# One pair's transposes moved from TensorE to DMA, and one sum of values moved to GpSimd, in a routed attention with a gated feed-forward

## The chip, the core and the metric

The kernel runs on one core of a Trainium2 chip. The metric is the device time of one execution in microseconds (us); a time is the median of several runs. The core has five instruction queues: PE (TensorE, matrix products), DVE (VectorE), ACT (ScalarE), POOL (GpSimd) and SP (SyncE, which here only issues DMAs). Each queue runs its own instructions strictly in the order in which they were built; queues wait for each other by semaphores.

## The reference

Four batches of eight heads, 768 positions, head size 64, sixteen centroids. Each query and key is assigned to its nearest centroid, and a query sees only keys of its own cluster. The result goes through a gated feed-forward.

```python
q_assign = argmax(einsum('bhsd,hcd->bhsc', q_n, c_n))      # k_assign in the same way
mask = q_assign[:, :, :, None] == k_assign[:, :, None, :]
scores = where(mask, scale * q @ k.T, -1e9)
attn_out = softmax(scores) @ v                             # (4, 8, 768, 64)
x = attn_out.transpose(0, 2, 1, 3).reshape(3072, 512)
out = (sigmoid(x @ w_gate) * (x @ w_val)) @ w_out          # (3072, 512) f32
```

## The kernel before

**Heads and tiles.** Heads are handled in pairs, four to a batch. For each head there is a tile `T` of 128 rows by 12 blocks of 128 columns: six blocks of keys, six of queries, each transposed. A number is stored as two f16 halves: `hi`, a cast, and `lo`, the f32 value minus `hi`; rows 0 to 63 of T hold hi and 64 to 127 lo. They stand in a tile `hl` first, not transposed. Once the cluster logits (`lg`, a product of T with the centroids `cm`) are taken, sixteen of the lo rows (64 to 79) are overwritten with the one-hot rows of the cluster (`oh`: for keys 1 at the cluster, for queries -1920 at every other one), so that one product of keys and queries gives a score with its mask already in it.

**Steps.** The attention runs in steps. One step is one score product `sc` (L1066, 128x384) on PE, one exponential `es` on ACT (L1071) and, two or three steps later, three products `av` (L1089) with the values `va`. After the last step of a pair DVE adds the sum of values `sv` and takes a reciprocal `rec` (L384, L389), POOL multiplies (`xp`, L390), and `xp` is turned to `xTb`, by PE (`x_ps`, L1117, copied by DVE at L1118) or by a DMA on SP (L1120). `sv` is 1e-30 times the column sum of the values, so that a query whose cluster holds no key gets their mean; the sum is made by a product with ones: either six products over `va` (`v_sum_pe`, L356) or three adds on f32 values and then one product (`v_sum`, adds L332, L338 and L339, product L343).

**The first batch** takes its queries in two halves of three blocks: the four pairs with the first half are steps 0 to 47, the same pairs with the second half are steps 48 to 95. Its preparation is done on PE (`first`, and `rest` for the second half of the queries: `hl2`, L1411 and L1415). From the second batch on, step 96 onwards, a pair takes 24 steps.

**Two ways to prepare a later pair.** `pieces` (L1159 to L1267) is the way on PE: the casts at L1171, the subtractions at L1178, twelve transposes a head by PE into `t_ps` (L1198), copied into T by DVE (L1211) or ACT (L1209), logits (L436), one-hots (L1226, L1229), six transposes a head for the one-hots into `oh_ps` (L1250), copied into T by DVE (L1261) and ACT (L1263). `pair_prep` is the way by DMA:

```python
DVE.tensor_copy(hl[:, :, 0:64], r)                                          # L1631
POOL.tensor_tensor(hl[:, :, 64:128], r, hl[:, :, 0:64], ALU.subtract)       # L1632
SP.dma_start_transpose(out=T[key], in_=hl.rearrange("p c x -> p (c x)"))    # L412
# logits L436, then on DVE: L451 (sum of two halves), L462 (max), L464 twice (one-hots), L471 (scale)
SP.dma_start_transpose(out=st["ot"], in_=st["oh"].rearrange("p c x -> p (c x)"))   # L1649
SP.dma_start(out=t[64:80, c0 : c0 + n, :], in_=src[32 * slot : 32 * slot + 16, 0:n, :])  # L492, four times
```

The number `npe` of the table `SCHED` says for how many pairs of the second batch the first way is taken: one, its first pair. All other pairs of the second to the fourth batch go by DMA.

**The feed-forward** of a block of 384 tokens is cut into groups of four products: `g` (L532, then a tanh `th` on ACT) and `v` (L548, then `hT` on DVE, L553), and after these the output products `o` (L865, L994). They are filled in between the steps by a credit in ns for each step (`ns..` in the table). The weights come by DMAs that POOL issues (L252, and L259 for `wo`).

**What sets the order.** Everything is written out by hand: `SCHED` holds, for each named piece of work, the step behind which it is built into the queues (for later batches as an offset from the first step of the pair, which is step 96 for the first pair of the second batch). PSUM has a ring of four banks that `sc`, `g`, `v`, `lg` and `x_ps` share: a product waits until the reader of the bank that it gets is done. `hl` has four buffers, T eight, the one-hot tile `oh` three.

Of the kernel before, what the change touches and what calls it, by code (L numbers as in the profile page):

```python
# [19 lines left out]
]  # L20
SCHED = {
# [74 lines left out]
    "fwv": [354, 356, 357, 359, 364, 366, 370, 371], "b3p2pk1": -28.5, "END": 0,  # L96
}


# [1671 lines left out]
```

## Time and profile before

| | |
|---|---|
| median of 3 runs | 319.33 us (319.31 to 320.36) |
| profiled execution | 319.12 us, of which the span from first to last instruction is 317.3 us |
| PE busy | 310.0 us (98%) |
| ACT, DVE, POOL busy | 244.9, 238.6, 120.9 us |
| step 48 / step 96 begin (sc) | 35.86 us / 73.36 us |
| granted TensorE clock | 1.00 |

The span's times count from its first instruction. A row of the timeline has start, duration, engine, line, operation, what is written from what, shapes, and how many follow each other; in brackets is how long the engine idled before and what ended it. Matmuls overlap in the pipeline, so a row's duration is longer than the time until the next one starts.

### The profile page before, as it was taken

What the parts mean: (1) busy time and instruction counts of PE and PEld (TensorE: products, weight loads), DVE (VectorE), ACT (ScalarE), POOL (GpSimd) and SP (SyncE); (2) the same over time, 40 slices, a digit from 0 to 9 for tenths busy, and PEclk for the clock granted to TensorE, in tenths of its full rate; (3) what the DMA queues carried; (4) which work ended last, traced back from release to release, by engine and by line L of the source; (5) the groups of instructions that cost most, each with busy time, mean ns of one, the idle gap of its engine ahead of it and who ended that gap; (6) DMA issues with size and microseconds to landing.
All of it is one profiled execution on the core that took longest, in us unless ns stands there. A gap on an engine that the chain in (4) does not pass through costs nothing.

```text
span 317.3 us, 9228 instructions
## 1 busy us (share of the span) xinstructions
PE 310.0 (98%) x3492; PEld 218.8 (69%) x3492; DVE 238.6 (75%) x623; ACT 244.9 (77%) x555; POOL 120.9 (38%) x157
## 2 busy tenths in 40 slices
PE   7899999999999999999999999999999999999995
PEld 4688766766666666666777678766677678656685
DVE  5899756778688777686788688776888776678983
ACT  6688998797899887877776876777877887588621
POOL 5888454244434275423234333424212111026600
PEclk9999999999999999999999999999999999999999
DMA  7999998639848988976676455882506130300014
GB/s 196 379 259 169 271 164 143 176 83 264 242 100 163 204 221 136 199 217 161 106 193 153 151 118 134 248 153 53 112 2 76 55 27 14 145 1 3 0 35 165
DMA packets 77996, 45.16 MB, mean 142 GB/s; under 512 B 56896, under 2 KB 75520, under 8 KB 77952
## 3 DMA queue, kind: packets, MB, share of 16 engines
q1 hardware_dynamic: 73840, 39.66, 51.3%
q0 software_dynamic: 3680, 4.72, 9.1%
q8 instruction: 27, 0.44, 0.6%
q10 hardware_dynamic: 432, 0.20, 0.2%
q14 instruction: 17, 0.14, 0.1%
HBM read 28.34 MB, written 6.29 MB: 109 GB/s over the span
## 4 chain that ended last, share of the span: by engine, by line
PE 93%; DMA 2%; DVE 1%; POOL 1%; SPq 1%; issue 0%; ACT 0%; DVEq 0%
PE sc L1066 19%; PE g L532 15%; PE v L548 15%; PE av L1089 11%; PE o L994 9%; PE o L865 5%; PE lg L436 2%; PE o L699 2%; PE o_end L802 2%; PE av L699 2%; DMA kraw<-in_k_dram 2%; PE v L628 2%; PE y L699 2%; PE o L802 1%; PE av L802 1%; PE z L699 1%
## 5 line engine op out<-in xcount | busy, mean ns | idle before, releaser
L1071 ACT ACTIVATE es<-sc 128x384 f16<-128x384 f32 x384 | 174.1, 492 | 38.5 <-PE sc L1066 29.8
L1066 PE MATMUL sc<-T 128*128 128x384 f16 x384 | 117.3, 325 | 0.7 <-DVE T L1396 0.4
L1089 PEld LDWEIGHTS <-es 128*128 128x128 f16 x1152 | 81.3, 98 | 35.1 <-ACT es L1071 0.2
L1089 PE MATMUL av<-va,es 128*128 128x65 f16 x1152 | 97.6, 194 | 0.0
L553 DVE SCALAR_TENSOR_TENSOR hT<-th,v 128x384 f16<-128x384 f32 x72 | 39.8, 553 | 33.8 <-PE av L1089 29.6
L377 POOL TENSOR_TENSOR xp<-t,rec 128x384 f16<-128x384 f32 (+1 forms) x30 | 21.8, 726 | 97.3 <-DVE rec L374 49.2
L548 PE MATMUL v<-xTb,wv 128*128 128x384 f16 x288 | 58.5, 326 | 0.1
L532 PE MATMUL g<-xTb,wg 128*128 128x384 f16 x288 | 58.5, 326 | 0.0
L538 ACT ACTIVATE th<-g 128x384 f32<-128x384 f32 x72 | 35.4, 492 | 8.3 <-PE g L532 6.3
L1066 PEld LDWEIGHTS <-T 128*128 128x128 f16 x384 | 37.0, 96 | 1.2 <-DVE T L1396 0.7
L548 PEld LDWEIGHTS <-wv 128*128 128x128 f16 x288 | 28.0, 97 | 13.9 <-issue 0.3
L532 PEld LDWEIGHTS <-wg 128*128 128x128 f16 x288 | 27.9, 97 | 13.9
L1632 POOL TENSOR_TENSOR hl<-kraw,hl 128x384 f16<-128x384 f32 x22 | 20.2, 920 | 40.6 <-DVE hl L1631 25.9
L1632 POOL TENSOR_TENSOR hl<-qraw,hl 128x384 f16<-128x384 f32 x22 | 21.1, 961 | 11.1 <-DVE hl L1631 11.1
L865 PE MATMUL o<-wo,hT 128*128 128x512 f16 x72 | 19.9, 379 | 0.0
L372 DVE TENSOR_TENSOR t<-av,sv 128x390 f32<-128x390 f32 (+1 forms) x30 | 14.4, 480 | 7.1 <-PE av L1089 5.3
L941 DVE TENSOR_TENSOR ob<-o,ob 128x256 f32<-128x256 f32 (+1 forms) x28 | 15.0, 549 | 4.7 <-PE o L994 3.2
L708 POOL TENSOR_TENSOR hT<-T 128x384 f16<-128x384 f32 x12 | 11.8, 1001 | 16.2 <-DVE T L657 15.6
L994 PE MATMUL o<-wo,hT 128*128 128x256 f16 x108 | 16.8, 272 | 0.0
L994 PEld LDWEIGHTS <-sum 128*128 128x128 f16 x144 | 14.0, 97 | 3.3
L451 DVE TENSOR_REDUCE lgs<-lg 128x192 f32<-128x384 f32 x23 | 12.7, 551 | 3.0 <-PE lg L436 2.9
L324 POOL CAST va<-vraw 128x768 f16<-128x768 f32 x15 | 13.1, 873 | 2.4 <-DMA vraw<-in_v_dram 2.4
(225 smaller groups left out, 470.2 us busy)
## 6 DMA issues: line engine op xcount, KB each, us to landing
vraw<-in_v_dram SPq DMA_DIRECT2D x15, 384.0 KB, 4.9
kraw<-in_k_dram SPq DMA_DIRECT2D x14, 384.0 KB, 4.2
qraw<-in_q_dram SPq DMA_DIRECT2D x12, 384.0 KB, 4.1
out_dram<-ob SPq DMA_DIRECT2D x17, 256.0 KB, 2.2
wg<-in_moe_w_gate_dram POOLq DMA_DIRECT2D x2, 768.0 KB, 9.2
wv<-in_moe_w_val_dram POOLq DMA_DIRECT2D x2, 768.0 KB, 10.4
wo<-in_moe_w_out_dram POOLq DMA_DIRECT2D x2, 768.0 KB, 9.3
T<-ohT SPq DMA_DIRECT2D x44, 24.0 KB, 1.9
```

Source lines behind the costliest of these rows:

```text
L377: (eng or POOL).tensor_tensor(x, t[:, 0:nq, 0:64], bcast(rec[:, 0:nq], 64), ALU.mult)
L532: PE.matmul(out=g[:, 0:n], lhsT=wg[fc // WQ][:, dc, fc % WQ, :], rhs=xT[:, dc, t0 : t0 + n], start=(dc == 0), stop=(dc == NDC - 1),)
L538: ACT.activation(th[:, 0:n], g[:, 0:n], AF.Tanh)
L548: PE.matmul(out=w[:, 0:n], lhsT=wv[fc // WQ][:, dc, fc % WQ, :], rhs=xT[:, dc, t0 : t0 + n], start=(dc == 0), stop=(dc == NDC - 1),)
L553: DVE.scalar_tensor_tensor(HB[b, blk][:, fc, 0:n], st[0][:, 0:n], 1.0, w[:, 0:n], ALU.add, ALU.mult)
L699: PE.matmul(out=o, lhsT=l, rhs=r, start=start and d == 0, stop=stop and d == 1, skip_group_check=True,)
L865: PE.matmul(out=o, lhsT=HB[b, blk][:, fc, bass.ts(t, 128)], rhs=wo[fc // WON][:, fc % WON, :], start=(fc == 0), stop=(fc == NFC - 1),)
L994: PE.matmul(out=st[z][:, e], lhsT=a[:, c, :], rhs=rhs[:, c, :], start=start and c + e == 0, stop=c == HF - 1, skip_group_check=True,)
L1066: PE.matmul(out=sc.rearrange("p (c t) -> p c t", t=128), lhsT=s["k"], rhs=s["q"], start=True, stop=True,)
L1071: ACT.activation(es, sc, AF.Exp, scale=SCALE)
L1089: PE.matmul(out=av[:, a0 + s["c0"] + i, :], lhsT=s["es"][:, bass.ts(i, 128)], rhs=VA[b, p][:, e, s["j"], :], start=(first and i == 0 and a ...
L1632: POOL.tensor_tensor(hl[:, :, 64:128], r, hl[:, :, 0:64], ALU.subtract)
```

## The change

Only the table `SCHED` changes.

```diff
-    "halved1": 1, "halved0": 4, "npe": 1, "npe0": 4, "vs00": 4.5, "gb": 0, "rb": 0, "h1hi0":
+    "halved1": 1, "halved0": 4, "npe": 0, "npe0": 4, "vs00": 4.5, "gb": 0, "rb": 0, "h1hi0":
...
-    75.5, "r3ot": 78.0, "r3pl0": 81.5, "r3pl1": 82.5, "ql3": -1, "vc03": 30.0, "vs03": 31.5,
+    75.5, "r3ot": 78.0, "r3pl0": 81.5, "r3pl1": 82.5, "ql3": -1, "vc03": 30.0, "vs03": 37,
...
-    "fwv": [354, 356, 357, 359, 364, 366, 370, 371], "b3p2pk1": -28.5, "END": 0,
+    "fwv": [354, 356, 357, 359, 364, 366, 370, 371], "b3p2pk1": -28.5, "b1p0sp00": -38, "b1p0sp01": -37, "b1p0sp10": -36, "b1p0sp11": -35, "b1p0tn0": -33.5, "b1p0tn1": -31, "b1p0lg0": -26, "b1p0pk0": -25, "b1p0lg1": -22, "b1p0pk1": -21, "b1p0ot": -19.5, "b1p0hp0": -13, "b1p0hp1": -12, "vd3": 1, "vq3": 1, "vt03": 6, "END": 0,
```

With `npe` at 0 the first pair of the second batch goes by DMA as well: 24 transposes of `hl` and 12 of `oh` leave PE, two T transposes, a one-hot transpose and four row copies are added to SP's queue. Its splits stand at steps 58 to 61 (before, 68 to 85), its transposes at 62.5 and 65, its logits at 70 and 74. `vd3`, `vq3` and `vt03` make the sum of values of the first batch's last pair by three adds on POOL and one product at step 43, where six products on PE stood at step 31.5.

The first place is POOL's queue around the xp of the first pair's second half (the first L390 after the `wo` DMAs in each piece; it is the one that x_ps of step 66 reads). Before:

```order
L259 DMA wo_120<-in_moe_w_out_dram 128x6x512
L1411 COPY hl_1280<-qheld 128x6x64
L259 DMA wo_121<-in_moe_w_out_dram 128x6x512
L1632 TENSOR_TENSOR hl<-kraw,hl 128x6x64
L390 TENSOR_TENSOR xp<-t,rec 128x2x3x64
L1415 TENSOR_TENSOR hl_1280<-qheld,hl_1280 128x6x64
L1632 TENSOR_TENSOR hl<-qraw,hl 128x6x64
```

And in the change:

```order
L259 DMA wo_120<-in_moe_w_out_dram 128x6x512
L1632 TENSOR_TENSOR hl<-kraw,hl 128x6x64
L1411 COPY hl_1283<-qheld 128x6x64
L1632 TENSOR_TENSOR hl<-qraw,hl 128x6x64
L1632 TENSOR_TENSOR hl<-kraw,hl 128x6x64
L259 DMA wo_121<-in_moe_w_out_dram 128x6x512
L1632 TENSOR_TENSOR hl<-kraw,hl 128x6x64
L1632 TENSOR_TENSOR hl<-qraw,hl 128x6x64
L390 TENSOR_TENSOR xp<-t,rec 128x2x3x64
L1415 TENSOR_TENSOR hl_1283<-qheld,hl_1283 128x6x64
```

Four more subtractions stand ahead of xp, and the second `wo` DMA stands behind three of them. PE's queue has x_ps at the same place in both, right behind the score product of step 66.

The second place is DVE's queue at the same steps; the difference:

```order
-L553 TENSOR_SCALAR hT<-th,v 128x384 x2
-L1631 COPY hl<-kraw 128x6x64
+L553 TENSOR_SCALAR hT<-th,v 128x384
+L1631 COPY hl<-kraw 128x6x64
+L1631 COPY hl<-qraw 128x6x64
+L553 TENSOR_SCALAR hT<-th,v 128x384
+L1631 COPY hl<-kraw 128x6x64 x2
+L1631 COPY hl<-qraw 128x6x64
```

The casts that POOL's subtractions wait for stand behind the first and the second hT.

The third place is DVE's queue at steps 71 to 76, in the change, from an hT over the two one-hot chains of the turned pair (L451 to L471, into `oh_136`) to the next two hT's; the chain at L1451 and L1452 is that of the last pair's second half, and PE turns its result `oh_134`:

```order
L553 TENSOR_SCALAR hT<-th,v 128x384
L384 TENSOR_TENSOR t<-av,sv 128x390
L389 RECIPROCAL rec<-t 128x6
L453 TENSOR_TENSOR lgs<-lg,lglo 128x96
L451 TENSOR_REDUCE lgs<-lg 128x192
L462 TENSOR_REDUCE mx<-lgs 128x12
L464 TENSOR_TENSOR oh_136<-lgs,mx 128x6x16 x2
L471 TENSOR_SCALAR oh_136<-oh_136 128x6x16
L1451 TENSOR_REDUCE mx<-lgs 128x6
L1452 TENSOR_TENSOR oh_134<-lgs,mx 128x2x3x16
L553 TENSOR_SCALAR hT<-th,v 128x384 x3
```

Before, the same piece has no L451 to L471 between L453 and L1451:

```order
L553 TENSOR_SCALAR hT<-th,v 128x384
L384 TENSOR_TENSOR t<-av,sv 128x390
L389 RECIPROCAL rec<-t 128x6
L453 TENSOR_TENSOR lgs<-lg,lglo 128x96
L1451 TENSOR_REDUCE mx<-lgs 128x6
L1452 TENSOR_TENSOR oh_136<-lgs,mx 128x2x3x16
L553 TENSOR_SCALAR hT<-th,v 128x384
```

The other one-hot chain of the turned pair, with two casts of the next pair behind it, stands just ahead of this piece in the change, also between two hT's.

## The prediction

> **What bounds the kernel now.** I read the page first, its totals and its chain that ended last:
>
> ```profile
> PE 310.0 (98%) x3492; PEld 218.8 (69%) x3492; DVE 238.6 (75%) x623; ACT 244.9 (77%) x555; POOL 120.9 (38%) x157
> ...
> PE 93%; DMA 2%; DVE 1%; POOL 1%; SPq 1%; issue 0%; ACT 0%; DVEq 0%
> ```
>
> TensorE is busy 98% of the span and is 93% of the chain. Then I read the two stretches that the change touches, in the table by windows:
>
> ```profile
> 30.00:40.00 10.00, 9.51 (x165) 7.21 (x163) 7.13 (x22) 9.56 (x25) 4.63 (x7) 1.00 1.07 253
> ...
> 60.00:70.00 10.00, 10.00 (x121) 6.73 (x120) 8.15 (x24) 9.02 (x20) 3.55 (x4) 1.00 0.59 143
> ```
>
> Columns: length, then busy us of PE, PEld, DVE, ACT and POOL, then clock and DMA. From 40 us on TensorE never pauses, so every matmul removed there is time won, and every wait put on TensorE is time lost. At 30 to 40 us ScalarE (9.56) binds as much as TensorE (9.51). The order of each engine is fixed at build, so a wait cannot be stepped around.
>
> **What goes.** The grouped rows and the timeline of PE:
>
> ```profile
> L1198 PE MATMUL t_ps<-identh,hl 128*128 128x128 f16 x24 | 2.0, 219 | 0.0
> ...
> L1250 PE MATMUL oh_ps<-identh,oh 128*128 128x128 f16 x12 | 1.0, 219 | 0.0
> ```
> ```profile
> 28.27 0.51 PE L356 MATMUL vs_ps<-va,ones 128*128 128x130 f16 x6
> 28.62 0.33 PE L1117 MATMUL x_ps<-identh,xp 128*128 128x128 f16 x3
> ...
> 34.12 0.32 PE L1066 MATMUL sc<-T 128*128 128x384 f16 x1
> ...
> 55.19 0.50 PE L1198 MATMUL t_ps<-identh,hl 128*128 128x128 f16 x6
> 55.52 0.81 PE L548 MATMUL v<-xTb,wv 128*128 128x384 f16 x4
> ```
>
> Durations overlap in the pipeline, so the cost is from start to start: six transposes hold TensorE 55.52 - 55.19 = 0.33 to 0.34 us. The 24 + 12 = 36 removed cost 6 x 0.335 = **-2.01 us**, all in stretches where TensorE binds. [...] The rows say 0.056 us apiece at granted clock 1.00, and they decide. The logits matmuls (L436) stay, 24 of them; they only move.
>
> **The sum of values.** Six matmuls go, one comes: 0.35 - 0.06 = 0.29 us of TensorE at 28.3 us. In its place GpSimd does three adds, which no row shows on GpSimd; the nearest are its 128x384 subtract (0.91) and the same adds on VectorE (0.55 for the first). The first add fits into the 1.46 us that GpSimd idles before 32.66 (row below). The other two follow that xp, which ends at 33.48; at 0.3 to 0.45 apiece they end at 34.1 to 34.4. The single ones-matmul stands right before the score matmul of 34.12, so after a gain of 0.29 TensorE waits there 0.2 to 0.5, and ScalarE, back to back then, hides part of it. Bounds -0.3 to +0.3; I take **0**, as gain and wait are the same size.
>
> **The wait that comes: GpSimd.** What precedes the attention output xp of the first pair's second half on GpSimd:
>
> ```profile
> 32.66 0.82 POOL L390 TENSOR_TENSOR xp<-t,rec 128x384 f16<-128x384 f32 x1 [1.46 <-DVE rec L389]
> ...
> 37.76 0.82 POOL L390 TENSOR_TENSOR xp<-t,rec 128x384 f16<-128x384 f32 x1 [3.83 <-DVE rec L389]
> 38.54 0.91 POOL L1415 TENSOR_TENSOR hl<-qraw,hl 128x384 f16<-128x384 f32 x1
> 39.40 0.89 POOL L259 DMA_DIRECT2D wo<-in_moe_w_out_dram  x1
> 40.28 0.52 POOL L1411 CAST hl<-qheld 128x384 f16<-128x384 f32 x1
> 40.73 0.82 POOL L259 DMA_DIRECT2D wo<-in_moe_w_out_dram  x1
> 44.46 0.91 POOL L1632 TENSOR_TENSOR hl<-kraw,hl 128x384 f16<-128x384 f32 x1 [2.91 <-DVE hl L1631]
> 45.67 0.82 POOL L390 TENSOR_TENSOR xp<-t,rec 128x384 f16<-128x384 f32 x1 [0.30 <-DVE rec L389]
> 46.45 1.03 POOL L1415 TENSOR_TENSOR hl<-qheld,hl 128x384 f16<-128x384 f32 x1
> ```
>
> Start to start a subtract takes 0.86, a wo load 0.88, the cast 0.45. In the changed order the xp now at 45.67 stands behind five subtracts, the cast and the second wo load. All of them follow the first of the new VectorE casts, which stands behind the first hT:
>
> ```profile
> 41.41 0.56 DVE L553 SCALAR_TENSOR_TENSOR hT<-th,v 128x384 f16<-128x384 f32 x1 [2.03 <-PE av L1089]
> 43.55 0.55 DVE L553 SCALAR_TENSOR_TENSOR hT<-th,v 128x384 f16<-128x384 f32 x1 [1.58 <-PE av L1089]
> 44.02 0.35 DVE L1631 CAST hl<-kraw 128x384 f16<-128x384 f32 x1
> ...
> 52.56 0.35 DVE L1171 CAST hl<-qraw 128x384 f16<-128x384 f32 x1
> 52.83 0.35 DVE L1631 CAST hl<-kraw 128x384 f16<-128x384 f32 x1
> ```
>
> A cast starts 0.47 after an hT (43.55 to 44.02) and GpSimd 0.44 after the cast's start (44.02 to 44.46): 41.41 + 0.47 + 0.44 = 42.32. Then 5 x 0.87 + 0.45 + 0.85 = 5.65: xp starts at 47.97 and ends at 48.79. TensorE needs it for x_ps:
>
> ```profile
> 38.64 0.34 PE L1117 MATMUL x_ps<-identh,xp 128*128 128x128 f16 x3
> ...
> 46.90 0.33 PE L1117 MATMUL x_ps<-identh,xp 128*128 128x128 f16 x3
> ```
>
> The earlier pair shows the coupling: xp 37.76 + 0.82 = 38.58, x_ps at 38.64, 0.06 later. Here x_ps can start at 48.85 instead of 46.90: **+1.95 us**. Bounds: 1.7 (each link a little shorter) to 2.6 (each subtract 1.03, as the one at 46.45). Queued behind x_ps is all of TensorE.
>
> **The second wait: VectorE.** The two logits blocks of the turned pair come at steps 70 and 74 instead of 79 and 92, so both one-hot chains and two casts fall between two hT. Rows for the pieces:
>
> ```profile
> 54.15 0.55 DVE L553 SCALAR_TENSOR_TENSOR hT<-th,v 128x384 f16<-128x384 f32 x1 [0.70 <-PE av L1089]
> 54.62 0.56 DVE L384 TENSOR_TENSOR t<-av,sv 128x390 f32<-128x390 f32 x1
> ...
> 56.44 0.55 DVE L553 SCALAR_TENSOR_TENSOR hT<-th,v 128x384 f16<-128x384 f32 x1
> ...
> 62.77 0.56 DVE L451 TENSOR_REDUCE lgs<-lg 128x192 f32<-128x384 f32 x1
> ...
> 64.31 0.55 DVE L553 SCALAR_TENSOR_TENSOR hT<-th,v 128x384 f16<-128x384 f32 x1
> ```
> ```profile
> 51.17 0.81 PE L548 MATMUL v<-xTb,wv 128*128 128x384 f16 x4
> ...
> 53.23 0.81 PE L548 MATMUL v<-xTb,wv 128*128 128x384 f16 x4
> ...
> 67.44 0.45 PE L436 MATMUL lg<-cm,T 128*128 128x32 f16 x12
> 67.74 0.32 PE L1066 MATMUL sc<-T 128*128 128x384 f16 x1
> ```
>
> One chain (reduce, max, two one-hots, scale) takes 64.31 - 62.77 = 1.54; the chain t, reciprocal, sum, max, one-hot 56.44 - 54.62 = 1.82; casts 0.27 apart (52.56 to 52.83); an hT 0.47. An hT follows its v by 0.92 (53.23 to 54.15). Count from the v that stands at 53.23. The hT before it began 2.06 earlier, so this one begins at -2.06 + 0.92 + 0.47 + 1.54 + 0.54 = 1.41 instead of 0.92, and ends at 1.96. After it come 0.47 + 1.82 + 1.54, so the rest rows' one-hots (oh) end at 5.24. TensorE gets to its transpose of them (oh_ps) at 4.17: it adds g and v (0.65 each), sc 0.165, av 0.09, and the block of 12 logits 0.30. With 0.06 for the semaphore it waits 5.30 - 4.17 = **+1.13**, part of it already at the g that needs the late hT's bank. Bounds 0.6 (VectorE 10% quicker) to 1.6 (10% slower).
>
> **The queue of SyncE.** The turned tiles themselves are in time: issued near 44.6 and 48.0, landing 3.8 us later, used near 52.9 and 56.3. Later the next pair's second tile is late: its transpose follows an xT transpose, three loads and now the one-hot transpose too.
>
> ```profile
> 59.33 2.42 SPq L412 DMA_TRANSPOSE T<-hl  x1
> ```
> ```profile
> T<-hl SPq DMA_TRANSPOSE x4, 3.8
> ```
> ```profile
> T<-hl SPq DMA_TRANSPOSE x1, 6.2
> ```
>
> (The 3.8 is the median of 20 to 60 us, the 6.2 the one behind three loads.) Its xp moves by about 3.0 us with VectorE, the added transpose is about 1.2: issue at 63.5, landing at 69.7. The logits that read it (67.44) move by 1.95 + 1.13 + 0.30 for a logits block that comes forward, less 4 x 0.335 removed by then, to 69.5. **+0.2**, bounds 0 and 0.9.
>
> **Sum.** -2.01 + 0 + 1.95 + 1.13 + 0.2 = +1.3. The profiled execution took 319.12 (span 317.3 and 1.8 around it), 0.2 below the median of 319.33; added to the median: **320.6**. Four evictions leave ScalarE and four VectorE; TensorE waits for none of them now, so that is worth nothing. All low bounds at once give 319.3 and all high ones 322.7; as they hardly fall together, the forecast's own range is 319.6 to 321.7.
>
> **Rivals.** *The waits stay hidden*: only the 2.0 are left, 317.3. For it: GpSimd idles 2.91 before 44.46 and the four added subtracts cost 3.5, which nearly fits. Against: the casts stand behind hT, so 0.9 of that idle time cannot be used, and the slack between xp and x_ps is only 46.90 - 46.49 = 0.4. Chance 0.13.
>
> *The late tile decides, slower*: the place is the block of logits at 67.44, which reads the next pair's second tile. SyncE issues the transpose of that tile behind the xT transpose, three loads and the added one-hot transpose. The price is 1 us for each us that it lands after 69.5, so it decides once the transpose is issued after about 63.3 (69.5 - 6.2). With 1.0 to 1.8 for loads that now share the transfer engines with one transpose more: 321.6 to 322.4. Against: only 0.2 is worked out above. Chance 0.17.
>
> *GpSimd is blocked by VectorE*: the subtract at 46.45 took 1.03 beside a busy VectorE against 0.91 elsewhere. If each of the five loses a whole hT or cast (0.35 to 0.55), the chain grows by 1.7 to 2.7: 322.3 to 323.3. Against: no row has more than 0.25 of it. Chance 0.08. [...]
>
> That the change does not do what it says is excluded by the built order.
>
> **How the numbers follow.** Forecast 0.62, hidden 0.13, late tile 0.17, blocked 0.08. A measurement of this kernel can tell 0.5%, 1.6 us, from no change: 317.7 to 320.9. A third of the forecast's band lies above 320.9. Faster 0.13; slower 0.17 + 0.08 + 0.21 = 0.46; the same 0.41. The range leaves out the hidden case and the far end of the others: 318.8 to 322.4.
>
> **What would show it.** TensorE's waits should have a new row of about 2 us at x_ps, L1117, for xp, L390, near 47 us, and 1 us of waits for VectorE at g and oh_ps near 57 to 61 us; busy PE falls by about 2. If x_ps starts within 0.5 us of its old place after sc, the GpSimd step is wrong; if the VectorE chain ends before oh_ps is reached, that step is. [...]

## The result and the profile after

The changed kernel takes **323.87 us** (median of 6 executions, 321.77 to 325.40) against 319.32 (318.80 to 320.36): a ratio of 1.0137, 95% interval 1.0090 to 1.0184. It is slower, above the range of 318.8 to 322.4. The profiled execution took 322.40, its span is 320.6 (before: 319.12 and 317.3).

The six executions fall in two groups by mean granted clock. Two ran at 1.000 (322.40 and 321.77, mean 322.1), four at 0.994 to 0.995 (323.06 to 325.40, mean 324.6). The profile below is one of the first group: the second has a cost of its own, which experiments 2, 8 and 11 show.

The page of the profile after, its totals and its chain:

```profile
PE 308.8 (96%) x3451; PEld 216.5 (68%) x3451; DVE 238.4 (74%) x621; ACT 241.8 (75%) x550; POOL 124.2 (39%) x161
...
PE 84%; DMA 5%; POOL 4%; issue 2%; DVE 2%; ACT 1%; SPq 1%; DVEq 0%; POOLq 0%
```

TensorE has 41 matmuls fewer, but the part of the chain on it fell from 93% to 84%: DMA, GpSimd and VectorE now end waits. What TensorE waits for (total, times, longest):

```profile
PE lg L436 <- DMA T<-hl: 1.7, 2, 1.4
PE x_ps L1117 <- POOL xp L390: 1.6, 1, 1.6
...
PE sc L1066 <- DVE hT L553: 0.6, 1, 0.6
...
PE vs_ps L343 <- ACT es L1071: 0.2, 1, 0.2
PE g L532 <- ACT th L538: 0.2, 1, 0.2
```

None of these five rows exists before. The three long ones in TensorE's timeline:

```profile
47.15 0.32 PE L1066 MATMUL sc<-T 128*128 128x384 f16 x1 [0.62 <-DVE hT L553]
...
47.40 0.33 PE L1066 MATMUL sc<-T 128*128 128x384 f16 x1
49.33 0.34 PE L1117 MATMUL x_ps<-identh,xp 128*128 128x128 f16 x3 [1.60 <-POOL xp L390]
...
56.78 0.23 PE L436 MATMUL lg<-cm,T 128*128 128x32 f16 x3
58.43 0.54 PE L436 MATMUL lg<-cm,T 128*128 128x32 f16 x15 [1.42 <-DMA T<-hl]
```

The start of the same score product, after minus before, is a running account of what the change has cost (us):

| step | 32 | 44 | 65 | 67 | 72 | 75 | 84 | 100 | 188 | end |
|---|---|---|---|---|---|---|---|---|---|---|
| shift | -0.29 | -0.11 | 0.67 | 2.38 | 2.81 | 4.70 | 3.52 | 2.64 | 3.04 | 3.3 |

The -0.29 stands from step 20 on, ahead of everything that the change moves, so up to step 44 the sum of values costs 0.18. Each later jump is one wait and a little more: 0.78 for the wait of 0.62, 1.71 for the one of 1.60. Of the 0.43 between 67 and 72, 0.30 is the first block of logits that comes forward. Of the 1.89 between 72 and 75, 1.42 is the wait and 0.30 the second block. Behind step 75 the 36 transposes that are gone (2.0) and the two blocks of logits that already ran (0.6) give back 2.06, 0.55 less than they should: 0.35 of that is lost at the g behind step 85 (67.67), which waits 0.18 for ScalarE's `th`, and 0.12 at the logits at 71.04, whose tile lands at 70.99.

**GpSimd's chain** ahead of xp, its queue in order of time:

```profile
42.21 0.95 POOL L1632 TENSOR_TENSOR hl<-kraw,hl 128x384 f16<-128x384 f32 x1 [2.04 <-DVE hl L1631]
43.11 0.50 POOL L1411 CAST hl<-qheld 128x384 f16<-128x384 f32 x1
43.57 0.91 POOL L1632 TENSOR_TENSOR hl<-qraw,hl 128x384 f16<-128x384 f32 x1
44.77 0.96 POOL L1632 TENSOR_TENSOR hl<-kraw,hl 128x384 f16<-128x384 f32 x1 [0.29 <-DVE hl L1631]
45.68 0.86 POOL L259 DMA_DIRECT2D wo<-in_moe_w_out_dram  x1
46.56 0.92 POOL L1632 TENSOR_TENSOR hl<-kraw,hl 128x384 f16<-128x384 f32 x1
47.44 0.91 POOL L1632 TENSOR_TENSOR hl<-qraw,hl 128x384 f16<-128x384 f32 x1
48.30 0.97 POOL L390 TENSOR_TENSOR xp<-t,rec 128x384 f16<-128x384 f32 x1
```

It begins at 42.21 (forecast 42.32) and reaches xp at 48.30 (forecast 47.97).

**VectorE beside it**, in the same microseconds and once later:

```profile
44.88 1.07 DVE L1631 CAST hl<-qraw 128x384 f16<-128x384 f32 x1
...
46.57 0.53 DVE L553 SCALAR_TENSOR_TENSOR hT<-th,v 128x384 f16<-128x384 f32 x1
...
47.18 1.42 DVE L1631 CAST hl<-qraw 128x384 f16<-128x384 f32 x1
...
56.91 0.35 DVE L1631 CAST hl<-kraw 128x384 f16<-128x384 f32 x1
```

A cast of 0.35 (56.91, GpSimd idle) takes 1.07 and 1.42 here. Each ends 0.2 to 0.25 after a GpSimd operation ends (45.73, 48.35). The hT behind the first of them is late, and sc at 47.15 waits for it: a wait that was not in the prediction.

**SyncE's queue**: the turned pair's second transpose (L412) and the first transpose of the last pair's second half (L1422), after; then L1422 before:

```profile
48.37 3.37 SPq L412 DMA_TRANSPOSE T<-hl  x1
...
51.84 1.21 SPq L1422 DMA_TRANSPOSE T<-hl  x1
```

```profile
47.51 1.28 SPq L1422 DMA_TRANSPOSE T<-hl  x1
```

The issue of a transpose holds SyncE for 3.37 us where the others from 44 to 56 us hold it 1.2 to 1.7, and L1422 stands behind it: issued 4.3 us later than before. The logits of the last pair's second half (3 + 3 matmuls, the x3 at 56.78 and the first three of the x15) are what waits 1.42: the second L1422, issued at 53.09, lands at 58.38, where before it landed at 52.25.

### The profile page after: what moved, and what is told of

It reads as the page before. It is cut to its first block, busy times and chain, and to the rows that moved or that the text cites. A ratio compares the mean times of both kernels' runs of the same rounds, so it can differ in the third digit from the quotient of the medians.

```text
span 320.6 us, 9159 instructions
## 1 busy us (share of the span) xinstructions
PE 308.8 (96%) x3451; PEld 216.5 (68%) x3451; DVE 238.4 (74%) x621; ACT 241.8 (75%) x550; POOL 124.2 (39%) x161
## 4 chain that ended last, share of the span: by engine, by line
PE 84%; DMA 5%; POOL 4%; issue 2%; DVE 2%; ACT 1%; SPq 1%; DVEq 0%; POOLq 0%
PE sc L1066 17%; PE g L532 13%; PE v L548 13%; PE av L1089 9%; PE o L994 9%; PE o L865 4%; DMA T<-hl 4%; PE o L699 2%; PE lg L436 2%; PE o_end L802 2%; PE av L699 2%; DMA kraw<-in_k_dram 2%; PE v L628 2%; PE y L699 2%; PE o L802 1%
## 5 line engine op out<-in xcount | busy, mean ns | idle before, releaser
L1632 POOL TENSOR_TENSOR hl<-kraw,hl 128x384 f16<-128x384 f32 x24 | 22.2, 926 | 40.5 <-DVE hl L1631 25.3
L1632 POOL TENSOR_TENSOR hl<-qraw,hl 128x384 f16<-128x384 f32 x24 | 22.9, 955 | 11.4 <-DVE hl L1631 11.4
L451 DVE TENSOR_REDUCE lgs<-lg 128x192 f32<-128x384 f32 x23 | 12.7, 552 | 1.9 <-PE lg L436 1.8
```

## The experiments

Three theories were to be told apart for the waits. **Queues**: each wait comes from one named queue position. **Full engines**: VectorE, SyncE and GpSimd have no room here, and a wait that is removed only moves. And for the clock: **a pause of TensorE of about 2 us makes the granted clock fall**, or chance does. Each run's own kernel before, on the same chip, had a median between 318.8 and 319.4.

### 1. The sum of values alone, in the kernel before

```diff
-    "vs03": 31.5,
+    "vs03": 37, "vd3": 1, "vq3": 1, "vt03": 6,
```

> Only the sum of values on GpSimd, the pair as before. My account (the loss comes from the pair's splits ahead of xp on GpSimd): TensorE gains 0.3 us at the place of the six matmuls and gives it back where it waits for the adds or ScalarE, so within 0.5 us of the kernel before, x_ps of step 66 within 0.3 us behind xp, granted clock 1.00 in all runs. Rival (the adds on GpSimd delay what follows them): 1 us or more slower, with a wait before the first hT.

319.28 us (10 executions), ratio 1.0009 (0.9997 to 1.0021). The product waits 0.2 for ScalarE. The gain of 0.25 at step 33 is gone at step 44, where the kernel is 0.17 later than at step 32 (0.18 in the change). So this part costs 0.2 us or less, within the bounds of the forecast.

### 2. The turned pair alone

```diff
-    "vs03": 37, "vd3": 1, "vq3": 1, "vt03": 6,
+    "vs03": 31.5,
```

> Only the pair's move, the sum of values back on TensorE. My account: the same three waits as in the change (0.6 for an hT, 1.6 at x_ps, 1.4 at the logits), so 3 to 3.5 us slower than before where the granted clock is 1.00, and about 1.6 more in executions where it is 0.995. Rival (the sum on GpSimd is part of the cause): no more than 1.5 us slower.

324.06 us (323.29 to 325.27, 4 executions), ratio 1.0168 (1.0141 to 1.0195): the whole loss is here. The waits for hT (0.62) and at x_ps (1.61) are those of the change; the one at the logits near 59 is 0.63 instead of 1.42, since TensorE comes there later. The profiled execution has a clock of 0.994; its windows (columns as in the prediction; clock is the third number from the right):

```profile
48.00:49.00 1.00, 0.00 (x0) 0.00 (x0) 0.97 (x3) 0.31 (x1) 1.00 (x2) 1.00 0.79 97
49.00:50.00 1.00, 0.80 (x7) 0.56 (x8) 0.71 (x2) 0.00 (x0) 1.00 (x2) 0.90 1.33 153
50.00:51.00 1.00, 1.00 (x7) 0.53 (x6) 0.46 (x1) 0.04 (x1) 1.00 (x3) 0.50 0.87 117
51.00:52.00 1.00, 1.00 (x5) 0.46 (x4) 0.10 (x1) 0.45 (x1) 0.76 (x1) 0.50 0.90 105
52.00:53.00 1.00, 1.00 (x7) 0.60 (x6) 0.00 (x0) 0.71 (x2) 0.00 (x0) 0.50 1.20 184
53.00:54.00 1.00, 1.00 (x14) 0.68 (x12) 0.23 (x1) 0.32 (x2) 0.00 (x0) 0.89 1.49 168
```

Right behind the pause the clock is halved for about 3.4 us, which loses 0.10 + 1.50 + 0.11 = 1.7 us. And a second tile comes late, that of the next pair, at the logits that stand at 67.44 before:

```profile
73.49 0.47 PE L436 MATMUL lg<-cm,T 128*128 128x32 f16 x12 [1.64 <-DMA T<-hl]
```

### 3. The second wo load out of GpSimd's chain

```diff
-    "wo1": 60.5,
+    "wo1": 56,
```

> The change with the second wo load issued five steps earlier, ahead of all splits, as it stood before. My account: the chain ahead of xp is shorter by one issue (0.86), so the wait at x_ps falls from 1.6 to about 0.8, and the transposes of T no longer share the transfer engines with that load: the wait of 1.4 us at the logits goes, and VectorE's chains take its place with 0.5 to 1.1. Together 1.2 to 2.2 us faster than the change at clock 1.00. Rival (the transposes are slow by themselves or because of the loads of q, k and v): the wait at the logits stays above 1.0 and the gain is 0.8 or less.

322.35 us (321.35 to 323.43, 4 executions), ratio 1.0112 (1.0083 to 1.0140). x_ps waits 0.83 instead of 1.60: close to the issue of 0.86 that left the chain. But of the 1.2 to 2.2 us expected less than 0.8 came (321.35 and 321.73 against 322.1), as the rival had it: the logits now wait twice for T, 0.87 and 0.92, and the second transpose of the turned pair holds SyncE 5.29 us instead of 3.37. A gain at one place, given back at another; the second wo load, issued at 45.68 in the change, is issued before 41.4 here, so that the two wo transfers (8.8 from issue to landing in the change) run at the same time, which put them under suspicion.

### 4. The splits behind xp

```diff
-    "b1p0sp00": -38, "b1p0sp01": -37, "b1p0sp10": -36, "b1p0sp11": -35, "b1p0tn0": -33.5, "b1p0tn1": -31,
-    "b1p0lg0": -26, "b1p0pk0": -25, "b1p0lg1": -22, "b1p0pk1": -21, "b1p0ot": -19.5, "b1p0hp0": -13, "b1p0hp1": -12,
+    "b1p0sp00": -33, "b1p0sp01": -32, "b1p0sp10": -31, "b1p0sp11": -30, "b1p0tn0": -28.5, "b1p0tn1": -26,
+    "b1p0lg0": -20.5, "b1p0pk0": -19.5, "b1p0lg1": -17, "b1p0pk1": -16, "b1p0ot": -14.5, "b1p0hp0": -10, "b1p0hp1": -9,
```

> The change with the pair's four splits put five steps later, behind the xp that x_ps reads, and its transposes, logits and one-hots 4.5 to 5.5 steps later too. My account: x_ps follows its score product without a wait, the hT before it as well, so of the 3.3 us that the change lost at least 2.3 come back; if the logits meet a landed tile, TensorE keeps the 2.0 us of the removed transposes: 1 to 2 us faster than the kernel before, clock 1.00 in all runs. Rival (DMA transposes cost TensorE time wherever they stand): still 1 us or more slower than before.

320.75 us (318.45 to 322.57, 10 executions), ratio 1.0049 (1.0016 to 1.0082). Expected was 1 to 2 us faster than the kernel before; it is slower, and two of the ten executions had a clock of 0.995. The waits at x_ps, for hT and for T near 58 are gone; two others came:

```profile
PE v L548 <- DVE oh L464: 1.5, 1, 1.5
...
PE sc L1066 <- DVE xTb L1118: 1.2, 1, 1.2
```

The second is the blocked cast again: casts of 1.07 and 1.06 (46.32 and 48.20, beside GpSimd) stand ahead of the copy of xTb. The first stands behind a cast that waits 3.6 for a load, issued 3.2 later than before, because the row copies of the turned pair hold SyncE until their one-hot tile has landed.

### 5. The second transpose behind L1422

```diff
-    "b1p0tn1": -31,
+    "b1p0tn1": -29,
```

> The change with one number altered: the turned pair's second transpose stands at step 67 instead of 65, so that on SyncE the two transposes of the last pair's second half (L1422) stand ahead of it. Theory (order of SyncE's queue): the 1.4 us at the logits are a wait for L1422's tiles, which stand behind a transpose that waits for GpSimd's last subtract; now they are issued right after GpSimd's L1415, near 50.2 instead of 51.84, and the wait at the logits is under 0.4; x_ps still waits 1.6 and sc 0.6 for hT; 1.0 to 1.4 us less than the change at the same clock. Rival (the landings are slow beside the wo load, whatever the order): a wait of 1.0 us or more for T stays at the logits, and the time stays within 0.5 of the change.

323.94 us (321.72 to 325.83, 4 executions), ratio 1.0155 (1.0114 to 1.0196). L1422 is issued at 50.49, both its tiles have landed by 56.45, and the wait near 58 is gone, as the queue theory has it. It would be gone at full clock too: in the change TensorE asked for the tile at 57.0. The sum did not fall: the profiled execution had the halved clock (0.995), and a wait of 1.47 came at the next pair's logits at 73.59. The one execution at 1.000 took 321.72, no better than the change there (321.77 and 322.40), and one at 0.999 took 323.05. With the landing wait gone, VectorE's lateness shows: a wait of 0.5 at g for hT.

### 6. The subtracts on VectorE

```diff
-            POOL.tensor_tensor(hl[:, :, 64:128], r, hl[:, :, 0:64], ALU.subtract)
+            (DVE if (b, p) == (1, 0) else POOL).tensor_tensor(hl[:, :, 64:128], r, hl[:, :, 0:64], ALU.subtract)
```

> The change with the turned pair's four subtracts on VectorE instead of GpSimd. Theory (GpSimd's chain delays x_ps, and GpSimd's running operation blocks VectorE's casts): xp starts within 0.5 us of its place before, the wait at x_ps is under 0.3, no cast near 44 to 48 us takes over 0.6, and the wait of sc for hT is no longer than the 0.6 of the change although VectorE has four operations more; transposes are issued earlier, so the logits wait less than 0.5; time 1.8 to 3.3 us below the change, 319.5 to 321, and the granted clock 0.998 or more in all runs, as the pause is gone. Rival (VectorE is full there, and the cost only moves to it): waits for VectorE of 1.5 us or more in sum replace the one at x_ps, time as the change.

322.14 us (321.74 to 323.57, 4 executions), ratio 1.0110 (1.0085 to 1.0134): above what was expected, 319.5 to 321. Right was that the wait at x_ps goes and that no cast is stretched; no execution is under 0.998. Wrong was the rest: hT and rec are late behind four more operations on VectorE (sc waits 1.04), and the turned tiles, now issued earlier and beside both wo transfers, hold SyncE for 6.08 us (46.66) and make the logits wait 0.99 and 0.92. The one subtract that had GpSimd beside it was stretched like a cast:

```profile
44.32 0.56 DVE L1632 TENSOR_TENSOR hl<-kraw,hl 128x384 f16<-128x384 f32 x1
...
45.45 1.15 DVE L1632 TENSOR_TENSOR hl<-qraw,hl 128x384 f16<-128x384 f32 x1
```

### 7. The casts on ScalarE

```diff
-            DVE.tensor_copy(hl[:, :, 0:64], r)
+            (ACT.copy if (b, p) == (1, 0) else DVE.tensor_copy)(hl[:, :, 0:64], r)
```

> The change with the turned pair's four casts on ScalarE instead of VectorE. Theory (a cast on VectorE cannot run while GpSimd works): the same casts take about 0.5 us each on ScalarE even beside a running subtract, the wait of sc for hT (0.6) is gone, the waits at x_ps (1.2 to 1.7) and for T at the logits (1.0 to 1.5) stay; 0.3 to 0.9 us less than the change at the same clock. Rival (the casts are slow for another reason that holds on any engine, such as the raw tile they read): ScalarE's casts take 0.9 us or more too, and the wait of sc stays or becomes one for ScalarE.

323.02 us (322.88 to 324.08, 4 executions), ratio 1.0136 (1.0115 to 1.0157). The same casts, beside the same subtracts:

```profile
44.66 0.56 ACT L1631 CAST hl<-kraw 128x384 f16<-128x384 f32 x1
...
45.46 0.56 ACT L1631 CAST hl<-qraw 128x384 f16<-128x384 f32 x1
```

ScalarE does them in 0.50 to 0.56, and the wait of sc for hT is gone. So it is VectorE's casts that GpSimd stops, not the cast or its input. The 0.3 to 0.9 expected did not come: ScalarE is busy all of this stretch, its exponentials come later, and steps 64 and 65 are 1.3 to 1.5 behind, with a longest wait of 0.44 for an exponential. x_ps still comes at 49.88 (waiting 1.35), as xp sets its time whether hT is late or not. The logits wait 1.63 for T.

### 8. Only a pause, in the kernel before

```diff
+        seen[b, p] = seen.get((b, p), 0) + 1
+        for _ in range(4 if (b, p) == (0, 0) and seen[b, p] == 2 else 1):
             POOL.tensor_tensor(
```

> The kernel before with one thing added: xp of the first pair's second half is multiplied four times over on GpSimd (the same values), so that x_ps comes 2.5 us later, less the 0.4 of slack: a pause of TensorE of about 2.1 us and nothing else. Theory (a pause of this length makes the granted clock fall to half for some 3.4 us in part of the executions): times from 321.4 up to 323.3, some at a mean clock of 0.994 to 0.996 with rows near 50 us at a clock of 0.50. Rival (the pause alone does not do it): clock 1.00 in all, all times within 0.5 us of 321.4.

322.06 us, ratio 1.0098 (1.0075 to 1.0120). One wait of over 1 us was added, 2.19 at x_ps for xp. Six executions: 321.40, 321.50 and 321.52 at a clock of 1.000; 322.60, 323.10 and 323.13 at 0.993 to 0.995. The windows of one of these:

```profile
48.00:49.00 1.00, 0.00 (x0) 0.00 (x0) 0.00 (x0) 0.00 (x0) 0.92 (x2) 1.00 1.23 205
49.00:50.00 1.00, 0.76 (x7) 0.57 (x8) 0.36 (x1) 0.00 (x0) 1.00 (x2) 1.00 1.14 189
50.00:51.00 1.00, 1.00 (x8) 0.55 (x7) 0.55 (x1) 0.28 (x1) 1.00 (x3) 0.57 0.17 26
51.00:52.00 1.00, 1.00 (x8) 0.54 (x6) 0.00 (x0) 0.21 (x1) 0.69 (x1) 0.50 0.43 98
52.00:53.00 1.00, 1.00 (x7) 0.50 (x5) 0.00 (x0) 0.94 (x2) 0.00 (x0) 0.50 0.38 85
53.00:54.00 1.00, 1.00 (x12) 0.60 (x11) 0.18 (x1) 0.04 (x2) 0.00 (x0) 0.72 0.10 19
```

0.43 + 0.50 + 0.50 + 0.28 = 1.7 us lost at a reduced clock; the two groups differ by 1.5 on average. A pause of 2.2 us is enough, in half the executions.

The traces also show what decides between the halves. The granted clock changes only at certain times: in each trace with a halved stretch every change lies a whole number of 3.41 us after the first one. Here the clock rises at 5.77, falls at 50.14 (13 x 3.413 later) and rises again at 53.55. Cut at these times, the stretch reads (columns of busy us as in the prediction, clock third from the right; then the same for the change, whose first rise is at 4.46):

```profile
46.73:50.14 3.41, 1.22 (x15) 0.70 (x13) 1.08 (x3) 1.10 (x3) 3.25 (x5) 1.00 1.14 187
50.14:53.55 3.41, 3.41 (x18) 1.73 (x17) 0.55 (x1) 1.47 (x3) 1.55 (x2) 0.50 0.28 61
```

```profile
45.42:48.83 3.41, 1.68 (x21) 0.94 (x17) 3.34 (x8) 2.02 (x5) 3.39 (x5) 1.00 1.22 162
```

A fall follows a window of 3.41 us in which TensorE was busy for 1.59 us or less (eight falls, in experiments 2, 5, 8, 9, 11 and 12), and none follows one with 1.68 or more; the change's profile, with both its waits, just kept its clock. Near the kernels' ends two windows with 1.45 and 1.60 (the kernel before and this one) had no fall behind them, so the limit is not sharp for all work. An estimate from it: a pause of 2.2 us puts the needed 1.8 us of idle time into one window from about 60% of its possible places, a pause of 4.0 from all. Where a pause falls against the windows differs from execution to execution (the first rise lies at 5.77 here, at 4.46 in the change and at 10.90 in experiment 12), and that part is luck.

### 9. Both wo loads early

```diff
-    "wo0": 54.5, "wo1": 60.5,
+    "wo0": 45, "wo1": 46.5,
```

> The change with both wo loads built at steps 45 and 46.5 instead of 54.5 and 60.5, ahead of the turned pair's work and into GpSimd's idle time near 34 to 37 us. Theory (the two 768 KB loads share the transfer engines with the turned tiles: the second turned transpose holds SyncE until the first is through, and the last pair's L1422 stands behind it): the second transpose of the turned pair, issued near 47.5, holds SyncE for under 2.2 us instead of 3.4, L1422 follows before 50.5, and the logits near 57 wait under 0.4 for T; x_ps waits 0.4 to 1.0, because one wo issue leaves GpSimd's chain; sc still waits 0.6 for hT; a wait of up to 0.9 may come at the next pair's logits near 70. Time 319.8 to 321.3 where the clock stays. Rival (a second transpose of this size holds SyncE whatever else is moved): it stays there for 3 us or more, and the logits wait 1 us or more, as in the run with the second load alone put early.

337.51 us (334.67 to 337.95, 4 executions), ratio 1.0557 (1.0520 to 1.0594). A filler product at step 46 reads the wo tile, and waits until the load that now overwrites it has landed:

```profile
46.93 0.29 PE L1063 MATMUL sc<-wo 128*128 128x128 f16 x1 [11.49 <-DMA wo<-in_moe_w_out_dram]
```

Neither theory expected that; the other reader was overlooked. The time says nothing, but the stretch behind it does. From 51.77 to 85.91 the clock is 1.00, and both wo loads, whole, have landed (at 46.88 and 50.67) before the turned tiles go out. The second turned transpose and the next pair's logits:

```profile
61.33 1.41 SPq L412 DMA_TRANSPOSE T<-hl  x1
```

```profile
85.05 0.47 PE L436 MATMUL lg<-cm,T 128*128 128x32 f16 x12 [1.90 <-DMA T<-hl]
```

The two turned transposes land 3.27 and 3.25 after their issue, the second holds SyncE 1.41, L1422 is issued 1.9 after xp starts, and the logits near 69 do not wait: what the theory said of the transfers came true, at full clock and with loads of full size (though hardly anything else was in flight either). x_ps waits 0.83, sc 0.62 for hT, and a g 0.48 for hT. The next pair's tile, behind three loads, is 1.90 late.

### 10. A mixed version

```diff
-    "wo1": 60.5, ... "b1p0sp10": -36, "b1p0sp11": -35, "b1p0tn0": -33.5, "b1p0tn1": -31,
-    "b1p0lg0": -26, "b1p0pk0": -25, "b1p0lg1": -22, "b1p0pk1": -21, "b1p0ot": -19.5, "b1p0hp0": -13, "b1p0hp1": -12,
+    "wo1": 56, ... "b1p0sp10": -30.5, "b1p0sp11": -29.5, "b1p0tn0": -28.5, "b1p0tn1": -26,
+    "b1p0lg0": -20.5, "b1p0pk0": -19.5, "b1p0lg1": -18, "b1p0pk1": -17, "b1p0ot": -15.5, "b1p0hp0": -5, "b1p0hp1": -4.5,
-            DVE.tensor_copy(hl[:, :, 0:64], r)
+            (ACT.copy if (b, p, e) == (1, 0, 1) else DVE.tensor_copy)(hl[:, :, 0:64], r)
```

> A version from what the runs showed: the change with the first head's splits as they are, the second head's splits behind xp with their casts on ScalarE, both transposes behind the last pair's L1422, the second wo load at step 56, the logits at steps 75.5 and 78, the one-hot transpose at 80.5 and the row copies behind the xT transpose. If the causes are named rightly: waits of under 0.3 at x_ps, at sc for hT and xTb, and for T at the logits near 55 to 58; no granted clock under 0.998; 317.3 to 318.6, 0.3 to 0.6% below the kernel before. If SyncE and VectorE are simply full in this stretch: waits of 1 to 2 us in sum come back further on (row copies before step 96, or v behind a cast that waits for a load), and the time is 319 or more.

320.27 us (319.48 to 322.15, 12 executions), ratio 1.0041 (1.0024 to 1.0058). Expected were 317.3 to 318.6. The waits at x_ps, for hT and for xTb are gone, that for T near 58 is 0.34, and at step 100 the kernel is 0.51 **ahead** of the one before. Then another tile, of a later pair, comes late:

```profile
95.05 0.47 PE L436 MATMUL lg<-cm,T 128*128 128x32 f16 x12 [1.48 <-DMA T<-hl]
```

Its transpose, right behind three loads on SyncE, held the queue 3.78 us and took 8.3 to land. So the second reading came true: a wait comes back further on. One execution of twelve had a clock of 0.995.

### 11. A longer pause

```diff
-        for _ in range(4 if (b, p) == (0, 0) and seen[b, p] == 2 else 1):
+        for _ in range(6 if (b, p) == (0, 0) and seen[b, p] == 2 else 1):
```

> The kernel before with xp of the first pair's second half multiplied six times over, a pause of TensorE of about 3.8 us (5 x 0.83 less 0.4). Theory (a long enough pause makes the granted clock fall, and whether one of 2.2 us is long enough depends on where it falls): now every execution has a mean clock of 0.993 to 0.996, and the time is 319.3 + 3.8 + 1.1 to 1.7 = 324.2 to 324.8 with a spread under 0.7. Rival (the fall is chance, independent of the pause's length): half the executions near 323.1 at clock 1.00, half near 324.8.

x_ps waits 4.0; all four executions are under 0.996 (0.995 three times, 0.984 once): 324.78 to 325.88, ratio 1.0202 (1.0176 to 1.0227). The level and the spread of 1.1 are above what was expected. 0 of 4 executions kept the clock at a pause of 4.0, 3 of 6 at 2.2, and 0 of 4 behind the 11.5 of experiment 9; halves by chance alone would give four of four once in 16. In the profiled execution the halved stretch is 3.41 long (51.54 to 54.95), as in experiments 2, 5 and 8. Such a stretch makes a mean clock of 0.995, and 0.984 stands for about three (an estimate: 1.7 us lost of 323 is 0.005).

### 12. The wo loads cut to a sixth

```diff
-            out=wo[i],
-            in_=moe_w_out.rearrange("(g fc p) m -> p g fc m", g=WOP, p=128)[:, i],
+            out=wo[i][:, 0:1],
+            in_=moe_w_out.rearrange("(g fc p) m -> p g fc m", g=WOP, p=128)[:, i, 0:1],
```

> The change with each of the two wo loads cut to its first sixth, 128 KB instead of 768 (the other five sixths are zeros, written by VectorE at the very start, so the feed-forward's output is left out in part and the first microseconds are up to 3 us longer; only the stretch of the turned pair is read). Nothing else differs in order. Theory (the wo transfers slow the turned tiles): the turned pair's second transpose holds SyncE for under 2.2 us instead of 3.37, the first lands within 4.2 us, L1422 is issued over 1 us earlier against xp than in the change, and the logits' wait of 1.42 for T falls under 0.4; x_ps still waits 1.3 to 1.8 and sc 0.6. Rival (a second transpose of this size holds SyncE until the first is done, whoever else uses the engines): 3 us or more on SyncE, and 1 us or more at the logits.

Only the stretch counts here, not the time (327.62). The two transposes in question, and from issue to landing of the three L414 here, the turned pair's two and the next pair's first (least, median, most):

```profile
49.17 1.41 SPq L414 DMA_TRANSPOSE T<-hl  x1
...
50.81 1.18 SPq L1424 DMA_TRANSPOSE T<-hl  x1
...
DMA to landing us min/median/max: 3.2/3.3/3.3
```

(L414 and L1424 are L412 and L1422, two lines further down.) The second transpose holds SyncE 1.41 instead of 3.37 and lands in 3.3 instead of 7.9. L1422 is issued 1.7 after xp starts instead of 3.5, and the wait near 58 is gone. It is the wo transfers that slow the turned tiles, as experiment 9 agrees; a transpose of this size alone holds the queue for 1.41 here. With that wait gone, VectorE's shows here too:

```profile
61.43 0.81 PE L534 MATMUL g<-xTb,wg 128*128 128x384 f16 x4 [0.48 <-DVE hT L555]
```

x_ps waits 1.18, a little under the 1.3 expected, and sc 0.62. Two waits came that neither theory held. The logits near 76 wait 2.43 for the next pair's tile, which lands 8.3 after its issue behind three loads of q, k and v; so loads other than wo slow a transpose too. And a g waits 1.22 for xTb, whose copy stands behind this cast:

```profile
48.25 2.76 DVE L1633 CAST hl<-qraw 128x384 f16<-128x384 f32 x1
```

GpSimd works without a break from 47.35 to 50.78, and the cast ends 0.23 after that: it got through only when GpSimd stopped.

### 13. The mixed version, one load later

```diff
+    "b2p0lk": 8, "b2p0lq": 8.5, "b2p0lv": 9,
-    "vs03": 37, "vd3": 1, "vq3": 1, "vt03": 6,
+    "vs03": 31.5,
```

> The mixed version with two things more: the loads of the third batch's first pair stand 8.5 steps later, behind the T transpose that they slowed (3.8 us on SyncE, 8.3 to landing, a wait of 1.5 at the logits near 95), and the sum of values is left on TensorE as before. If that late tile is all that stands between the mixed version and the kernel before: no wait for T over 0.3, and 318.3 to 319.0, level with the kernel before or up to 0.3% faster. If the stretch simply has no room on SyncE: another tile, load or row copy comes late by 1 us or more, and the time is 319.8 or more.

319.59 us (318.48 to 321.99, 12 executions), ratio 1.0018 (0.9992 to 1.0044): level with the kernel before, not faster. Expected were 318.3 to 319.0, or 319.8 and more; it lies between. The tile near 95 is in time, but logits still wait for T in two places (0.60 and 0.56) and v 0.36 for a one-hot chain. The best of these versions gives back the 2.0 us of transposes in the queues; none beat the kernel before.

## Why the prediction was wrong, point by point

Slower had the largest chance (0.46), but not by these mechanisms: the forecast of 320.6 is 1.5 below the executions at full clock (322.1) and 3.3 below the median. That 322.1 lies inside the range of 318.8 to 322.4 is luck: a wait of 1.13 that was in the sum did not come, and one of 1.42 that was not in it did.

| term | forecast | measured |
|---|---|---|
| transposes gone | -2.0 | within 2.06 given back behind step 75, where 2.6 was to be had |
| sum of values | 0 | +0.18 (steps 32 to 44; 0.17 in experiment 1) |
| x_ps for xp | +1.95 | +2.43 (46.90 to 49.33), the wait for hT included |
| VectorE's one-hot chains | +1.13 | 0 in the change; 0.5 once nothing hides it |
| next pair's tile | +0.2 | +0.12 there, a wait of 0.27 further on; waits of 1.5 to 2.4 in experiments 2, 5, 9 and 12 |
| late tile of L1422 | none | 1.42, with its tail 1.6 |
| halved clock | none | 1.5 to 1.7 where it falls; 4 of 6 executions |

1. **"Then 5 x 0.87 + 0.45 + 0.85 = 5.65: xp starts at 47.97"** was near: 48.30. x_ps came at 49.33 against a forecast of 48.85, since GpSimd waited 0.29 for one of VectorE's slow casts (44.77) and xp took 0.97 instead of 0.82. The chain was rightly named and sized within 0.5, and experiments 3 and 6 take out one link and all four subtracts with the wait that belongs to them.

2. **"GpSimd is blocked by VectorE"** had the coupling the wrong way round. The rival looked for GpSimd's rows to grow; they hardly did (a subtract 0.91 to 0.96). It is VectorE's cast that stops until a GpSimd operation is done (0.35 to 1.07 and 1.42 in the change, while ScalarE's stay at 0.50 to 0.56 in experiment 7; 2.76 in experiment 12), and what that delays is hT, which no term held. Its wait of 0.62 does not add to the one at x_ps, though: x_ps cannot start before xp is through at 49.27, so with hT in time it would have waited that much longer; in experiment 7, where the wait for hT is gone, it still waits 1.35 for xp. Why it is VectorE that stops and not GpSimd, no run shows.

3. **"The turned tiles themselves are in time"** is true, and was the wrong question. The first landed 4.7 after its issue, the second 7.9 (forecast 3.8 for each), both before their logits. The step that failed is SyncE's queue: L1422, which already stood there, was moved behind the second transpose, and no term priced that: 1.42 at the logits, 1.6 with its tail. The second transpose waits for GpSimd's last subtract (48.35), then holds the queue 3.37 us, because the second wo load is on the transfer engines (experiments 9 and 12). The prediction's rows of before hid this: a landing of 3.8 was a median over other company.

4. **VectorE's 1.13** was in the sum and did not happen: TensorE, held 1.42 for the tile, came to oh_ps after the chain was done. Two waits one behind the other do not add. Where the tile is in time (experiments 5, 9 and 12), 0.5 of it appears, at g.

5. **The halved clock** was in no term and no rival. It adds 2.5 between the two groups of executions (322.1 and 324.6): 1.7 by the clock itself, and in the profile of experiment 2 the next pair's tile late by 1.64 on top, less 0.79 that the logits near 59 wait less. That tile is the prediction's "late tile" rival, at its place and near its price (1.0 to 1.8, the author's estimate). It needs no halved clock, for it is 1.90 late in experiment 9 at 1.00. It landed 7.3 to 8.3 after its issue in experiments 2, 5, 9 and 12, but 5.8 to 6.7 in the change and experiments 3, 6 and 7; why is open. The clock comes back after 3.41 us at 0.50 (experiments 2, 5, 8, 11 and 12); it fell behind windows of 3.41 us with 1.8 or more of idle time (experiment 8). The windows do not start with the kernel: the clock's first rise lies anywhere from 4.46 us (the change) to 10.90 (experiment 12), and the later changes follow it in steps of 3.41.

6. What is left: the three waits cost 0.44 in sum beyond their own length, as the last matmul before a wait no longer overlaps the next (a score product lasts 0.32, but the next one starts 0.16 after it where nothing waits). The g that waits for `th` costs 0.35. About 0.5 of the 3.3 is not tied to a row. Busy PE fell by 1.2, not by the 2 that the prediction looked for.

## What to carry to other kernels

Work taken off the busiest engine is worth its time only if every queue that it moves to has that much slack just there (here 2.0 us left TensorE, and the profiled span grew by 3.3): list what stands behind each new instruction on each queue, transposes on the DMA queue first, and ask who reads it. Price a DMA by the company that it will have, not by a median over the profile (the turned pair's second transpose landed 7.9 us after its issue in the change and 3.3 in experiment 12). The pause of 2.2 us in experiment 8 cost 2.6 to 2.7 where the clock stayed and 3.8 to 4.3 where it was halved (against 318.79 before); so waits that fall into one window of 3.4 us are to be weighed as one. And before a wait is added to a sum, ask whether a later one on the same path hides it (with hT in time, the 1.60 at x_ps would have been longer by the 0.62).

## What the runs showed of the hardware

- A VectorE cast of 128x384 (f32 to f16) takes 0.35 us alone, 0.46 to 1.42 beside single operations of GpSimd (0.46 at 46.25 in the kernel before, 0.76 at 47.51 in experiment 7, 1.07 and 1.42 in the change) and 2.76 beside an unbroken row of them (experiment 12), ending 0.2 to 0.3 after one of them; VectorE's subtract takes 0.56, and 1.15 beside GpSimd (experiment 6). ScalarE's cast stays at 0.50 to 0.56 (experiment 7). GpSimd's own rows grow by up to 0.2 (xp 0.82 to 0.97 in the change, a subtract 0.91 to 1.12 in experiment 7).
- A transpose of 128x1536 by DMA lands 3.3 us after its issue with the weight loads done or cut to a sixth (experiments 9 and 12), 4.4 to 9.8 with one or two loads of 768 KB beside it (the change and experiments 3, 6, 7), where the second of two holds SyncE's queue for 3.4 to 6.1 us instead of 1.41 (experiments 9 and 12). Behind three loads of 384 KB it took 5.8 to 8.3 (6.7 in the change, 8.3 in experiments 10 and 12).
- Behind a pause of 2.2 us the mean clock was 0.993 to 0.995 in 3 of 6 executions (experiment 8), behind one of 4.0 under 0.996 in 4 of 4 (experiment 11); the traces show 0.50 for 3.41 us. The granted clock changes in steps of 3.41 us from its first rise, and it fell behind windows in which TensorE was busy for 1.59 us or less, not behind those with 1.68 or more (all traces, the kernels' ends left out). The kernel before, with no such pause, had a mean clock under 0.996 in 8 of its 64 executions beside the experiments; why in those is open.
